# A planned FP32 kernel (attention with state, then two expert layers): the plan in eight passes by deadlines, turns of w3 in a stream of their own, rows of state row by row

## The chip, the cores and the metric

The kernel runs on one core of one Trainium2 chip. Five engines of that core matter here. PE is TensorE: it does the matrix products, and its weight loads are listed apart as PEld. DVE is VectorE. ACT is ScalarE. SP is SyncE, which here only issues DMAs. POOL does next to nothing. Each engine works off its own list of instructions strictly in order, and an instruction that waits holds up all that stand behind it on the same engine.

The metric is device time in microseconds (us) of one execution. Before the change three runs gave 1343.75, 1333.1 and 1341.79 us, so the median is 1341.79 us. The profile below is of one further execution, which took 1337.37 us.

## What is computed

```
# x 8x8x512x64, state 8x8x32x64, all FP32
scores  = x @ state^T / 8 ;  a  = softmax(scores)  (over the 32 rows of state)
xread   = a @ state                                # 512 rows of each batch
scores2 = state @ x^T / 8 ;  a2 = softmax(scores2) (over the 512 rows of x)
sread   = a2 @ x                                   # 32 rows of each batch
x = concat(xread, sread)  ->  4608 rows (8 batches of 544) x 512
x = ((x @ w1) * (x @ w2)) @ w3 @ w_out             # 512 -> 1024 -> 1024 -> 512
h = x @ w_in ;  g = h - tanh(h) ;  out = g @ w_out2   # 512 -> 2048 -> 512
```

FP32 accuracy is kept by splitting a number into a high and a low part and taking three products of parts (high-high, high-low, low-high). The weights of the layers come as 64-bit floats, so each slice of a weight has to be unpacked to FP32 by ACT and DVE before it is used.

## The kernel before

**Two parts.** The first part, to about 584 us of the span, does the attention, the first layer and all unpacking of weights. Its instructions are put in order by a planner (class `Plan`, L44 to L141). The second part, from there to the end, is the second layer; its order is written out by hand (`stage3`, `stage4`, `curve`, `finish`).

**What the first part does.** The words used below are these.

- *Products of w3.* `w3 @ w_out` is made first, in 16 steps t = 0 to 15 (8 for each half h of w3's rows). A step has a *turn* (`w3_turn`: four 128x128 transposes on PE into a PSUM bank), a *copy* of the bank to SBUF by ACT (the tile `w3t`), and a *product* (`w3_mul`: four matmuls, L735, which add into the banks acc0 to acc3). After steps 7 and 15 ACT and DVE take the four banks out as high and low part (`w3o`).
- *Unpacking.* A slice takes two ACTIVATEs (`unpack_abs` L261 and `unpack_tail` L267; the second is on DVE for every other slice of w3) and three DVE instructions (L278, L283, L289). The slices of w1 and w2, in four pairs kk = 0 to 3 (`raw12`, `dt12`), are then split into high and low part (`w12`). The memory of the pairs kk = 2 and 3 is that of the unpacked w_out, which the products of w3 read: pair 2 can be fetched only when product 11 is done, pair 3 only when product 15 is.
- *Folds.* Instead of x @ w1 with the x that attention reads, the rows of state are multiplied into w1 and w2 (`fold` r, kk, q: six matmuls on PE into two banks; r = 0 for batches 0 to 3, r = 1 for 4 to 7). ACT and DVE copy the banks out (`fe`), SP stores them in DRAM (`mdr`), and later loads them as `m` for each batch b and step k (`load_m`, a ring of three).
- *Attention of batch b.* `scores` on PE, then softmax steps on ACT and DVE, `et` (transposes) and `sr` (products) on PE. They give `at[b]`. The 32 rows of state of each batch go through `srb`, a transpose `st` on PE and a copy `keep_sr` (L535) into the tile `xsr`; after batch 7, `xsr` is split into `atsr`, the block b = 8.
- *Stage 1 and stage 2.* For b in 0 to 6, 8, 7 and k in 0 to 7, stage 1 multiplies `at[b]` by `m` (PSUM banks `ab`, two units a step), ACT and DVE make `ac` and `ph` of them, and stage 2 multiplies `ph` by `w3o` (banks acc0 to acc3, named y, two units of two banks a step). After k = 7 ACT copies the four banks to `y`, and SP stores them to DRAM (`ydr`), where the second part fetches them. The rings of `ac` and `ph` are two and three, that of `y` is two.

**What sets the order.** Each piece of work is a *part* with an engine, an assumed duration, what it needs, what buffers it takes and gives back. Parts stand in streams; in a stream the parts of one engine stay in order. `run` (L119) walks once through all streams: it works out when each engine's next part of every stream could start, takes the engine with the earliest start, and among that engine's parts that could start within 250 ns of it takes the one whose stream has the lowest rank for this engine. Turn, copy and product of w3 stand in one stream (`x_s`, rank 3 on PE and 2 on ACT), so on PE turn t + 1 follows product t. Buffers in four PSUM banks are picked by the same walk.

## Time and profile before

| | before |
|---|---|
| median of three runs | 1341.79 us (1333.1 to 1343.75) |
| the profiled execution | 1337.37 us, span 1335.5 us |
| PE busy | 1282.8 us (96% of the span) |
| DVE busy | 978.2 us (73%) |
| ACT busy | 723.9 us (54%) |
| mean granted TensorE clock | 0.993 |
| bytes moved | 150.58 MB, mean 113 GB/s |

The span is what the profiler recorded from the first to the last instruction; 1.9 us of the execution's time lie outside it. Busy time of an engine is the sum of its instructions. An engine's idle time ahead of an instruction is put down to what released that instruction ("releaser"). Where PE is busy nearly all the time, work on the other engines costs nothing as long as it is ready when PE comes to it.

### The profile page before, as it was taken

What the parts mean: (1) busy time and instruction counts of PE and PEld (TensorE: products, weight loads), DVE (VectorE), ACT (ScalarE), POOL (GpSimd) and SP (SyncE); (2) the same over time, 40 slices, a digit from 0 to 9 for tenths busy, and PEclk for the clock granted to TensorE, in tenths of its full rate; (3) what the DMA queues carried; (4) which work ended last, traced back from release to release, by engine and by line L of the source; (5) the groups of instructions that cost most, each with busy time, mean ns of one, the idle gap of its engine ahead of it and who ended that gap; (6) DMA issues with size and microseconds to landing.
All of it is one profiled execution on the core that took longest, in us unless ns stands there. A gap on an engine that the chain in (4) does not pass through costs nothing.

```text
span 1335.5 us, 17513 instructions
## 1 busy us (share of the span) xinstructions
PE 1282.8 (96%) x6416; PEld 1005.6 (75%) x6416; DVE 978.2 (73%) x1638; ACT 723.9 (54%) x1172; POOL 0.7 (0%) x6
## 2 busy tenths in 40 slices
PE   6798999999999999999999999999999999999996
PEld 3345676767777689788888888888888888888886
DVE  7898786775655842559977687787876877768775
ACT  7788575564646622446555455454544545545454
...
GB/s 326 270 226 212 255 256 214 246 200 280 250 250 284 189 91 95 220 69 90 1 64 1 9 56 0 64 0 1 64 0 54 10 1 64 1 0 48 1 32 16
DMA packets 98286, 150.58 MB, mean 113 GB/s; under 512 B 13976, under 2 KB 68248, under 8 KB 96152
## 3 DMA queue, kind: packets, MB, share of 16 engines
...
## 4 chain that ended last, share of the span: by engine, by line
PE 73%; DMA 12%; DVE 5%; ACT 4%; SPq 4%; issue 1%; DVEq 0%; ACTq 0%
PE h_ps L250 26%; PE o_ps L1286 26%; PE ab_ps L250 9%; PE y_ps L1027 7%; DMA raw_w<-in_moe_w_in_dram 3%; DMA m<-mdr 2%; DMA raw_p<-in_moe_w_dram 2%; PE w3o_ps L735 2%; DMA raw_w<-in_moe_w_out_dram 1%; DMA mdr<-fe 1%; SPq L396 1%; SPq L974 1%; PE m_ps L877 1%; DMA raw_p<-in_moe_w_out_dram 1%; ACT raw L267 1%
## 5 line engine op out<-in xcount | busy, mean ns | idle before, releaser
L250 PE MATMUL h_ps<-yt,w2in 128*128 128x512 f32 (+1 forms) x1728 | 394.0, 377 | 0.0
L250 PEld LDWEIGHTS h_ps<-yt,w2in 128*128 128x128 f32 x1728 | 313.4, 188 | 61.1
L250 PE MATMUL ab_ps<-at,m 128*128 128x512 f32 x768 | 196.2, 404 | 14.1 <-ACT ac L220 4.2
L1027 PE MATMUL y_ps<-ph,w3o 128*128 128x512 f32 (+1 forms) x864 | 201.4, 381 | 3.0 <-ACT y L220 3.0
L250 PEld LDWEIGHTS ab_ps<-at,m 128*128 128x128 f32 x768 | 141.6, 191 | 60.0 <-ACT ac L220 13.9
L1027 PEld LDWEIGHTS y_ps<-ph,w3o 128*128 128x128 f32 x864 | 153.7, 188 | 39.4 <-issue 6.1
L223 DVE TENSOR_TENSOR ph<-ac,ph 128x512 fp32r<-128x512 f32 (+1 forms) x72 | 47.5, 660 | 85.8 <-ACT ph L220 84.8
L220 ACT ACTIVATE ph<-ac 128x512 fp32r<-128x512 f32 (+1 forms) x72 | 43.9, 610 | 104.6 <-PE y_ps L1027 91.7
L735 PE MATMUL w3o_ps<-wo,w3t 128*128 128x512 f32 x128 | 64.0, 646 | 12.6 <-ACT w3t L220 12.6
L735 PEld LDWEIGHTS w3o_ps<-wo,w3t 128*128 128x128 f32 x128 | 24.7, 203 | 43.0 <-issue 26.5
L1010 DVE TENSOR_TENSOR ac<-ab_ps,ac 128x512 f32<-128x512 f32 (+1 forms) x72 | 47.2, 655 | 4.7 <-PE ab_ps L250 4.5
L267 ACT ACTIVATE raw_w<-raw_w 128x512 uint16<-128x512 uint32 x32 | 43.6, 1362 | 0.6
L220 ACT ACTIVATE ac<-ab_ps 128x512 f32<-128x512 f32 (+1 forms) x72 | 40.4, 561 | 2.0 <-PE ab_ps L250 1.9
L1296 DVE COPY ob<-o_ps 128x512 f32<-128x512 f32 x17 | 11.8, 692 | 39.1 <-PE o_ps L1286 39.1
L261 ACT ACTIVATE dt_w<-raw_w 128x512 f32<-128x512 f32 x32 | 21.4, 668 | 32.0 <-DMA raw_w<-in_moe_w_in_dram 16.6
L223 DVE TENSOR_TENSOR m<-m 128x512 fp32r<-128x512 f32 x32 | 22.0, 688 | 22.3 <-ACT m L220 22.0
L220 ACT ACTIVATE fe<-m_ps 128x512 fp32r<-128x512 f32 (+1 forms) x48 | 28.1, 601 | 16.8 <-PE m_ps L877 7.6
L220 ACT ACTIVATE m<-m 128x512 fp32r<-128x512 f32 x32 | 20.2, 631 | 30.2 <-DMA m<-mdr 30.0
L220 ACT ACTIVATE ob<-o_ps 128x512 f32<-128x512 f32 x17 | 10.2, 599 | 45.0 <-PE o_ps L1286 45.0
L877 PE MATMUL m_ps<-w,uu 64*128 64x512 f32 x192 | 32.3, 427 | 2.0 <-DVE fe L900 1.2
L278 DVE TENSOR_SCALAR dt_w<-dt_w 128x512 f32<-128x512 f32 x32 | 13.4, 420 | 23.4 <-ACT dt_w L261 23.2
L877 PEld LDWEIGHTS m_ps<-w,uu 64*128 64x128 f32 x192 | 16.8, 184 | 16.8 <-issue 6.2
...
## 6 DMA issues: line engine op xcount, KB each, us to landing
...
m<-mdr SPq DMA_DIRECT2D x128, 128.0 KB, 4.6
xb<-in_x_dram SPq DMA_DIRECT2D x64, 128.0 KB, 3.6
...
m<-mdr SPq DMA_DIRECT2D x128, 64.0 KB, 2.7
...
```

Source lines behind the costliest of these rows:

```text
L220: nc.scalar.activation(dst, src, AF.Copy)
L223: nc.vector.tensor_tensor(out=lo, in0=src, in1=hi.bitcast(F32), op=ALU.subtract)
L250: nc.tensor.matmul(out_ap, lhs(i), rhs(j), start=(n == 0), stop=(n == m - 1))
L261: nc.scalar.activation(t.bitcast(F32), w[:, :, 1].bitcast(F32), AF.Abs)
L267: nc.scalar.activation(tail, w[:, :, 0], AF.Copy, scale=TAIL)
L278: nc.vector.tensor_scalar(out=t, in0=t, scalar1=EXP_LO, scalar2=EXP_HI, op0=ALU.max, op1=ALU.min)
L396: nc.sync.dma_start(xb[b][band(q, j), j].rearrange("p g c d -> p g (c d)"), x[b, 2 * q + j].rearrange("(g p c) d -> p g (c d)", p=NS, c=NC),)
L735: nc.tensor.matmul(acc[a], v[:, a * P:(a + 1) * P], wo[j][:, 512:].bitcast(F32), start=(j == 0), stop=(j == nj - 1),)
L877: nc.tensor.matmul(ts[j].rearrange("p (k f) -> p k f", k=2), uu[r][1][d, i, q * P:(q + 1) * P], w[d, :, l, q, :], start=(n == 0), stop=(n ...
L1010: nc.vector.tensor_tensor(out=ab[b, k], in0=ab[b, k, 1], in1=ab[b, k], op=ALU.mult)
L1027: nc.tensor.matmul(acc[o][:, :n], w3o[k // 4][:, k // 2 % 2, i, c + o * P:c + (o + 1) * P], p[:, j], start=(k == 0 and e == 0), stop=(k == ...
L1286: nc.tensor.matmul(acc[t], g[:, i, t * P:(t + 1) * P], w[:, l, c], start=(f == 0 and e == 0), stop=(f == NF - 1 and e == 2),)
```

## The change

There are three edits.

1. **The plan is made eight times.** The old `emit` is split into `place`, which notes the times of a part and what it had to wait for, and the issue of the instructions, which now comes at the end. A pass (`order`) is the old walk, with one difference: among the parts that can start within 250 ns, the one with the earliest *deadline* (`late`) goes first. In the first pass the deadlines are the old ranks. After each pass `justify` goes through the parts from the last to the first and pushes each as late as the parts behind it and the free time of its engine allow; these times are the deadlines of the next pass. Of the eight passes the one in which PE ends first, by the planner's assumed durations, is issued.
2. **Turns and copies of w3 get a stream of their own** (`t3_s`), with ranks a little ahead of those of the products, so that a turn can be put ahead of the product of the step before.
3. **The rows of state lie row by row.** `keep_sr` writes the 128 x 128 numbers of a batch to every eighth place of `xsr` instead of to a block, and the last output DMA of each group of 128 rows names rows of state first and batches second. The number of instructions and of bytes stays the same.

The number of instructions on each engine is the same before and after, except that runs of equal rows join differently. The diff, cut to its core:

```
--- before.py
+++ after.py
@@ -46,32 +46,39 @@
 
 
 
+
+
     NEAR = 250.0
     REACH = {"PE": 200.0, "ACT": 130.0, "DVE": 130.0, "SP": 0.0}
+    ROUNDS = 8
 
     def __init__(self):
-        self.free = dict.fromkeys(self.REACH, 0.0)
-        self.moved = 0.0
-        self.made, self.slots, self.held, self.streams = {}, {}, {}, []
-
-        self.banks = [([0, 0.0], None) for _ in range(4)]
+        self.rings, self.streams = {}, []
+
         self.most = {"ab": 4, "w3x": 4, "fold": 2, "ps": 2}
         self.picked = []
 
     def ring(self, name, n):
-        self.slots[name] = (n, [])
+        self.rings[name] = n
 
     def stream(self, rank, ahead=16):
         s = {"rank": rank, "ahead": ahead, "parts": []}
         self.streams.append(s)
         return s["parts"]
+
+    def clear(self):
+        self.free = dict.fromkeys(self.REACH, 0.0)
+        self.moved = 0.0
+        self.made, self.held = {}, {}
+        self.slots = {name: (n, []) for name, n in self.rings.items()}
+        self.banks = [([0, 0.0, []], None) for _ in range(4)]
 
     def start(self, p):
         t = self.free[p["eng"]]
         for n in p["need"]:
             if n not in self.made:
                 return None
-            t = max(t, self.made[n])
+            t = max(t, self.made[n][0])
         for name, _, _ in p["take"]:
             if name in self.most:
                 continue
@@ -92,53 +99,109 @@
             t = max(t, free[want - 1])
         return t
 
-    def emit(self, p, t):
+    def place(self, p, t):
+
         end = t + p["dur"]
         self.free[p["eng"]] = end
         if p["bytes"]:
             self.moved = max(self.moved, t + 600) + p["bytes"] / 300.0
             end = self.moved + 1600
         reach = end + self.REACH[p["eng"]]
+        p["after"] = [q for n in p["need"] for q in self.made[n][1]]
+        p["span"], p["lag"], p["banks"] = (t, t + p["dur"]), reach - t - p["dur"], []
         for name, key, uses in p["take"]:
-            slot = [uses, 0.0]
+            slot = [uses, 0.0, []]
             if name in self.most:
                 k = min((b[0][1], i) for i, b in enumerate(self.banks) if not b[0][0])[1]
+                p["after"] += self.banks[k][0][2]
                 self.banks[k] = (slot, name)
-                self.picked.append(k)
+                p["banks"].append(k)
             else:
-                self.slots[name][1].append(slot)
+                n, given = self.slots[name]
+                if len(given) >= n:
+                    p["after"] += given[len(given) - n][2]
+                given.append(slot)
             self.held[key] = slot
         for key in p["give"]:
             slot = self.held[key]
             slot[0] -= 1
             slot[1] = max(slot[1], reach)
+            slot[2].append(p)
         for n in p["make"]:
-            self.made[n] = max(self.made.get(n, 0.0), reach)
-        p["fn"]()
-
-    def run(self):
-        while True:
+            at, by = self.made.get(n, (0.0, []))
+            self.made[n] = (max(at, reach), by + [p])
+
+    def order(self):
+        self.clear()
+        found, lists = [], [list(s["parts"]) for s in self.streams]
+        while any(lists):
             can = []
-            for s in self.streams:
+            for s, parts in zip(self.streams, lists):
                 seen = set()
-                for k, p in enumerate(s["parts"][:s["ahead"]]):
+                for k, p in enumerate(parts[:s["ahead"]]):
                     if p["eng"] not in seen:
                         seen.add(p["eng"])
                         t = self.start(p)
                         if t is not None:
-                            rank = s["rank"].get(p["eng"], 9) if p["rank"] is None else p["rank"]
-                            can.append((t, rank, s["parts"], k, p))
+                            can.append((t, p["late"], parts, k, p))
             if not can:
-                left = [s["parts"][0] for s in self.streams if s["parts"]]
+                left = [parts[0] for parts in lists if parts]
                 assert not left, [(p["eng"], p["need"], p["take"]) for p in left]
-                return
             t0, _, _, _, p0 = min(can, key=lambda c: c[0])
             t, _, parts, k, p = min(
                 (c for c in can if c[4]["eng"] == p0["eng"] and c[0] <= t0 + self.NEAR),
                 key=lambda c: (c[1], c[0]),
             )
             del parts[k]
-            self.emit(p, t)
+            self.place(p, t)
+            found.append(p)
+        return found
+
+    def justify(self, found):
+
+        end = max(p["span"][1] for p in found)
+        gaps = {e: [(0.0, end)] for e in self.REACH}
+        bound = {id(p): end for p in found}
+        for s in self.streams:
+            last = {}
+            for p in s["parts"]:
+                if p["eng"] in last:
+                    p["after"].append(last[p["eng"]])
+                last[p["eng"]] = p
+        late = {}
+        for p in sorted(found, key=lambda p: -p["span"][1]):
+            free = gaps[p["eng"]]
+            k = next(
+                (
+                    k for k in reversed(range(len(free)))
+                    if min(free[k][1], bound[id(p)]) - free[k][0] >= p["dur"]
+                ),
+                0,
+            )
+            a, b = free[k]
+            t = min(b, bound[id(p)]) - p["dur"]
+            free[k:k + 1] = [(a, t), (t + p["dur"], b)]
+            late[id(p)] = t
+            for q in p["after"]:
+                lag = q["lag"] if q["eng"] != p["eng"] or q["bytes"] else 0.0
+                bound[id(q)] = min(bound[id(q)], t - lag)
+        for p in found:
+            p["late"] = late[id(p)]
+
+    def run(self):
+        for s in self.streams:
+            for p in s["parts"]:
+                p["late"] = s["rank"].get(p["eng"], 9) if p["rank"] is None else p["rank"]
+        best = None
+        for _ in range(self.ROUNDS):
+            found = self.order()
+            end = max(p["span"][1] for p in found if p["eng"] == "PE")
+            if best is None or end < best[0]:
+                best = end, [(p, p["banks"]) for p in found]
+            self.justify(found)
+        for p, banks in best[1]:
+            self.picked += banks
+            p["fn"]()
 
 
 @with_exitstack
@@ -534,7 +597,7 @@
 
             def keep_sr():
                 copy(
-                    xsr[:, :, b * NS:(b + 1) * NS],
+                    xsr.rearrange("p q (n b) -> p q n b", b=B)[:, :, :, b],
                     s["st"].rearrange("p (q n) -> p q n", q=KT),
                 )
 
@@ -667,6 +730,7 @@
         w12, raws, f32s, acc_w = {}, {}, {}, {}
         w3o, w3v, w3x = {}, {}, {}
         w_s = plan.stream({"ACT": 3, "DVE": 3, "SP": 0}, 40)
+        t3_s = plan.stream({"PE": 2.8, "ACT": 1.5, "DVE": 1.5}, 40)
         x_s = plan.stream({"PE": 3, "ACT": 2, "DVE": 2, "SP": 0}, 40)
         d_s = plan.stream({"PE": 4, "ACT": 4, "DVE": 4, "SP": 1}, 24)
 
@@ -776,11 +840,11 @@
                 )
             whole = [("f32", i, n) for n in range(2 if i < 2 else 1)]
             part(
-                x_s, "PE", 4 * TURN, later(w3_turn, t), whole[:1], [("w3x", t)],
+                t3_s, "PE", 4 * TURN, later(w3_turn, t), whole[:1], [("w3x", t)],
                 [("w3x", ("w3x", t), 1), ("w3t", ("w3t", t))], [("pdt", i)] if h else (),
             )
             part(
-                x_s, "ACT", ("scalar", 512), lambda t=t: copy(w3v[t], w3x[t]),
+                t3_s, "ACT", ("scalar", 512), lambda t=t: copy(w3v[t], w3x[t]),
                 [("w3x", t)], [("w3t", t)], (), [("w3x", t)],
             )
             part(
@@ -1297,9 +1361,10 @@
             else:
                 copy(ob[:, t], acc[t])
             if j == B:
-                nb = P // NS
+
+                c = S + t * (P // B)
                 nc.sync.dma_start(
-                    out.rearrange("(b s) o -> b s o", b=B)[nb * t:nb * (t + 1), S:], ob[:, t]
+                    out.rearrange("(b s) o -> s b o", b=B)[c:c + P // B], ob[:, t]
                 )
         if j < B:
             nc.sync.dma_start(
```

What the change moves is shown at three places, in rows of the built programs: line, operation, what is written, what is read, size, and how many equal ones follow each other.

On PE at the start of the program: `w3_ps` t is the bank of turn t, `w3o_ps0` 0 to 3 are the four banks of the products, `w3t` t is the turned tile. Before:

```order
L242 MATMUL w3_ps1_201<-ident_74,wo0_125 128x128 x4
L735 MATMUL w3o_ps0_0_177<-wo0_125,w3t1_206 128x512
L735 MATMUL w3o_ps0_1_179<-wo0_125,w3t1_206 128x512
L735 MATMUL w3o_ps0_2_181<-wo0_125,w3t1_206 128x512
L735 MATMUL w3o_ps0_3_183<-wo0_125,w3t1_206 128x512
L242 MATMUL w3_ps2_234<-ident_74,wo0_125 128x128 x4
```

Of the changed kernel:

```order
L305 MATMUL w3_ps1_204<-ident_74,wo0_125 128x128 x4
L305 MATMUL w3_ps2_229<-ident_74,wo0_125 128x128 x4
L799 MATMUL w3o_ps0_0_181<-wo0_125,w3t1_209 128x512
L799 MATMUL w3o_ps0_1_183<-wo0_125,w3t1_209 128x512
L799 MATMUL w3o_ps0_2_185<-wo0_125,w3t1_209 128x512
L799 MATMUL w3o_ps0_3_187<-wo0_125,w3t1_209 128x512
L305 MATMUL w3_ps3_250<-ident_74,wo0_125 128x128 x4
```

Turn 2 stands ahead of product 1 now, and so it goes on: turn t + 1 is ahead of product t up to product 6, and turns 8 to 11 are ahead of product 8.

On ACT around the unpacking and splitting of pair 3 of w1 and w2 (`raw12_6`, `dt12_7` are its slices, `w12_3` its split form; `fe0_2` are copies of folds, `ac`, `ph`, `m`, `a`, `e2t` as in the words above). Before:

```order
L267 ACTIVATE raw12_6_944<-raw12_6_944 128x512
L474 ACTIVATE a1_1_893<-a1_1_893 128x512
L220 ACTIVATE ph0_2_1116<-ac0_2_1094 128x512
L220 ACTIVATE e2t1_1_1119<-et_ps1_1_996 128x512
L220 ACTIVATE fe0_2_301_1128<-m_ps0_2_3_0_1107 128x512
L220 ACTIVATE w12_3_1130<-dt12_6_1005 128x4x128 x2
L220 ACTIVATE w12_3_1130<-dt12_7_1053 128x4x128 x2
```

Of the changed kernel:

```order
L283 ACTIVATE fe0_2_001_954<-m_ps0_2_0_0_907 128x512
L330 ACTIVATE raw12_6_800<-raw12_6_800 128x512
L283 ACTIVATE fe0_2_101_976<-m_ps0_2_1_0_956 128x512
L283 ACTIVATE ph0_1_987<-ac0_1_941 128x512
L283 ACTIVATE w12_3_992<-dt12_6_898 128x4x128 x2
L283 ACTIVATE fe0_2_201_1003<-m_ps0_2_2_0_978 128x512
L283 ACTIVATE w12_3_992<-dt12_7_944 128x4x128 x2
```

Before, ACT has taken up step 2 of batch 0 (`ph0_2`) by then, and step 3 follows; now it is at step 1 (`ph0_1`). On PE the changed kernel has, between product 15 and the first fold of pair 3, only folds 0_1 and 0_2 (eight), scores of batch 1 and stage 1 of steps 0 and 1 of batch 0 (four units); before, stage 1 of steps 0 to 3 and five units of stage 2 stand ahead of that fold too.

On PE where the rows of state of batch 7 are turned (`st_ps7`) and the block b = 8 begins (`ab_ps8`). Before:

```order
L242 MATMUL st_ps7_4697<-ident_74,srb7_4693 128x128
L250 MATMUL ab_ps6_6_0_4699<-at6_4322,m6_6_4543 128x512 x6
L250 MATMUL ab_ps6_6_1_4714<-at6_4322,m6_6_4543 128x512 x6
L250 MATMUL ab_ps6_7_0_4726<-at6_4322,m6_7_4574 128x512 x6
L250 MATMUL ab_ps6_7_1_4739<-at6_4322,m6_7_4574 128x512 x6
L1027 MATMUL y_ps6_0_4590<-ph6_2_4514,w3o0_418 128x512 x3
```

Of the changed kernel:

```order
L579 MATMUL sr_ps7_1_4786<-xn7_4056,e2t7_1_4771 32x64 x16
L1091 MATMUL y_ps6_0_4517<-ph6_7_4711,w3o1_1078 128x512 x3
L1091 MATMUL y_ps6_1_4521<-ph6_7_4711,w3o1_1078 128x512 x3
L1091 MATMUL y_ps6_2_4550<-ph6_7_4711,w3o1_1078 128x512 x3
L1091 MATMUL y_ps6_3_4554<-ph6_7_4711,w3o1_1078 128x512 x3
L305 MATMUL st_ps7_4836<-ident_74,srb7_4833 128x128
L313 MATMUL ab_ps8_0_0_4849<-atsr_4839,w12_0_456 128x256 x12
L313 MATMUL ab_ps8_0_1_4863<-atsr_4839,w12_0_456 128x256 x12
```

Before, seven units of batch 6 stand between `st_ps7` and `ab_ps8`; now nothing does.

## Rows read from the trace of the kernel before

**Rows 1.** Windows: from:to, us, then busy us (instructions) of PE, PEld, DVE, ACT, POOL; PEclk, DMA share, GB/s

```profile
112.78:138.46 25.68, 24.28 (x166) 17.54 (x166) 24.00 (x47) 20.41 (x34) 0.00 (x0) 1.00 0.70 228
138.46:583.70 445.24, 426.47 (x2491) 328.50 (x2491) 273.98 (x512) 232.45 (x393) 0.00 (x0) 0.99 0.70 209
583.70:1335.50 751.80, 741.74 (x3361) 617.10 (x3359) 585.54 (x921) 386.75 (x634) 0.00 (x0) 1.00 0.08 28
```

**Rows 2.** Waits, whole span: who waited for whom, us in total, times, longest

```profile
PE w3o_ps L735 <- ACT w3t L220: 12.6, 13, 4.2
```

**Rows 3.** Waits of PE from 138.46 to 583.7 us, same columns

```profile
PE ab_ps L250 <- ACT ac L220: 4.2, 6, 1.8
PE y_ps L1027 <- ACT y L220: 3.0, 2, 1.7
PE ab_ps L250 <- ACT at L220: 1.7, 1, 1.7
```

**Rows 4.** Timeline of PE: start, us, line, operation, tiles, count (idle before, releaser)

```profile
15.28 3.70 PE L735 MATMUL w3o_ps<-wo,w3t 128*128 128x512 f32 x8 [0.69 <-ACT w3t L220]
18.91 0.66 PE L242 MATMUL w_ps<-ident,wo 128*128 128x128 f32 x4
...
48.39 5.40 PE L735 MATMUL w3o_ps<-wo,w3t 128*128 128x512 f32 x8 [4.22 <-ACT w3t L220]
...
96.44 0.97 PE L877 MATMUL m_ps<-w,uu 64*128 64x512 f32 x6
97.34 1.95 PE L421 MATMUL sc_ps<-xt,ut 32*32 32x512 f32 x32
...
108.75 0.96 PE L877 MATMUL m_ps<-w,uu 64*128 64x512 f32 x6
...
131.08 0.65 PE L516 MATMUL sr_ps<-xn,e2t 128*32 128x64 f32 x32
...
138.46 0.96 PE L877 MATMUL m_ps<-w,uu 64*128 64x512 f32 x6
```

**Rows 5.** Timeline of PE, later: two units of stage 1; turn of batch 7's rows

```profile
384.26 3.06 PE L250 MATMUL ab_ps<-at,m 128*128 128x512 f32 x12
...
480.52 0.27 PE L242 MATMUL st_ps<-ident,srb 128*128 128x128 f32 x1
```

**Rows 6.** Timeline of ACT: unpacking of the first slices of w1, w2; two copies

```profile
44.06 0.68 ACT L261 ACTIVATE dt<-raw 128x512 f32<-128x512 f32 x1 [4.08 <-DMA raw<-in_moe_w_dram]
44.77 1.34 ACT L267 ACTIVATE raw<-raw 128x512 uint16<-128x512 uint32 x1
45.85 0.69 ACT L261 ACTIVATE dt<-raw 128x512 f32<-128x512 f32 x1
...
56.29 0.60 ACT L220 ACTIVATE w3t<-w_ps 128x512 f32<-128x512 f32 x1
56.78 0.59 ACT L220 ACTIVATE sc<-sc_ps 128x512 f32<-128x512 f32 x1
```

**Rows 7.** Timeline of DVE: end of w3's third slice; low parts of pair 3

```profile
17.62 1.23 DVE L289 SCALAR_TENSOR_TENSOR wo<-raw_p,wo 128x1024 uint32<-128x1024 uint32 x1 [2.47 <-ACT raw_p L267]
...
130.83 2.49 DVE L223 TENSOR_TENSOR w<-dt,w 128x512 fp32r<-128x512 f32 x4
```

**Rows 8.** Windows of product 7 and of four units after 451.9 us, columns as in Rows 1

```profile
48.39:53.72 5.33, 5.33 (x8) 2.03 (x9) 4.62 (x10) 5.07 (x7) 0.00 (x0) 0.68 1.09 348
...
451.90:456.42 4.52, 4.52 (x15) 3.28 (x13) 3.87 (x8) 1.87 (x4) 0.00 (x0) 0.62 1.03 376
```

**Rows 9.** The tile xsr: what writes and reads it; ns min/median/max, first and last start us

```profile
L220 ACT ACTIVATE xsr<-st_ps x8: 266/278/283, 78.5 to 481.7; 128x128 f32<-128x128 f32 x8
...
L223 DVE TENSOR_TENSOR atsr<-xsr,atsr x2: 686/690/694, 482.7 to 483.3; 128x512 fp32r<-128x512 f32 x2
```

**Rows 10.** DMA issues of the page: count, KB each, us to landing

```profile
m<-mdr SPq DMA_DIRECT2D x128, 128.0 KB, 4.6
```

**Rows 11.** The chain that ended last, in order of time: start, us, what

```profile
372.24 9.41 DMA m<-mdr
```

## The prediction

> **What bounds the kernel now.** I first cut the span into windows by what PE does [rows 1]. From 583.70 us to the end PE is busy 741.74 of 751.80 us. This is the second layer; its order is written by hand and the diff leaves it alone. So nothing is won there, and the 751.8 us stay. What the change can move lies before 583.7 us. From 138.46 to 583.70 PE is busy 426.47 of 445.24 us, so 18.8 us are idle while DVE (274) and ACT (232) have room: PE bounds that stretch, and its idle time is many small waits. From 112.78 to 138.46 DVE is busy 24.00 of 25.68 us and PE 24.28: there PE and DVE are both near full.
>
> Next I read who PE waits for. The largest sum is the products of w3 waiting for the copy of their own turn: 13 waits, 12.6 us [rows 2]. The timeline shows the pattern: a product of 3.63 us (15.28 to 18.91), a turn of 0.66, a wait of 0.69 for ACT; the longest such wait is the 4.22 us before the product at 48.39 [rows 4]. That product also ran slowly, 5.33 us at a mean granted clock of 0.68 [rows 8], so for most of it at 1.2 instead of 2.4 GHz: 1.7 us more than the one at 15.28. The four units of 451.90 (4.52 us at 0.62) did the same after a wait, against 3.06 us for as many matmuls at 384.26 [rows 5, 8]. In the later stretch the waits of stage 1 for `ac`, of stage 2 for `y` and for `at` are the largest [rows 3].
>
> **The sum, step 1: products 0 to 7.** Turn t + 1 now stands ahead of product t, so the copy has a whole product's time, and the 0.69 us go. At the start this costs something: product 1 waits behind turn 2, which needs w3's third slice. That slice's last DVE instruction began at 17.62 after waiting 2.47 us for ACT, which stood behind a copy [rows 7]; without the copy it can begin near 15.2, but the data of the next slices come in order, and I take turn 2 at 17.0. Then product 1 is at 17.7, product 2 at 17.7 + 3.63 + 0.66 = 22.0, and products 2 to 7 with a turn each take 6 x 4.29 = 25.7: product 7 ends at 47.7. Before it ended at 48.39 + 5.33 = 53.7. Gain here 6.0 us, 1.7 of them the clock.
>
> **Step 2: products 8 to 15.** PE's list up to product 15 is eight products (29.0), seven turns (4.6), scores of batch 0 (1.95), four folds (3.9), two et as long as a turn (1.3), two sr (1.3) and st (0.3): 42.3 us [rows 4, 5]. Waits: the fourth matmul of product 8 needs acc3 taken out, which on ACT stands behind four unpacked slices (44.06 + 4 x (0.71 + 1.08) + 5 copies x 0.49 + a low part of 0.7 = 54.4 [rows 6, 9]), when PE is there at 47.7 + 3 turns + 1.95 + 2.7 = 54.3; and turn 12 comes about 1.8 us before its slice is through. I take 2 us. Product 15 ends at 47.7 + 42.3 + 2 = 92.0; before at 108.75.
>
> **Step 3: the folds, where most of this is given back.** Pair 3 of w1 and w2 can be fetched only after product 15. Before, it was split 130.83 + 2.49 - 108.75 = 24.6 us later [rows 4, 7]. The same path (fetch, eight ACT instructions, three times four on DVE, the split) now starts at 92.0 and ends at 116.6. The order puts the first fold of pair 3 on PE behind only eight folds (7.8), scores (1.95) and four units of stage 1 (6.1), 15.9 us, so PE stands about 9 us. By 119.5 it has done that fold, an et and one more fold (0.97 + 0.66 + 0.97, 0.3 of waiting). Before, PE at 138.46 had done four units of stage 1 and five of stage 2 more (9 x 1.53 = 13.8), an et and two sr more (2.0), and two folds less (1.9): the same state as now at 138.46 - 13.9 = 124.6. **Gain up to here 5.1 us**, out of 16.7 at product 15. Bounds: 14 if the pair is ready as PE comes; 0 if ACT and DVE need 5 us more.
>
> The Trainium skill says in "Perfetto Trace Analysis", Optimization Strategy, that where the most-contended engine changes over time, interleaving the regimes may help. The new order does the opposite here: it packs the folds together, ahead of most of stages 1 and 2, and the trace has ACT and DVE full in that stretch [rows 1]. What this would do in full is rival B.
>
> **Step 4: 138.46 to 583.70.** The same instructions run for the same times; only waits can go, 18.8 us in all. Two I can follow. Stage 2 of batch 4 began on banks that `y` copies had not left (1.7 us); four units of stage 1 now stand between. Batch 6's stage 1 followed its last sr directly and waited for `at` (1.7) [rows 3], and then ran 4.52 - 3.06 = 1.5 us longer at the low clock; `at` has far more time now. That is 4.9 us. Of the other 15.4 us I cannot say which the new order removes. None is the one bound, all the other; I take a third, 5.1, since of what I could follow nearly all goes, but stage 1's waits for `ac` come from ACT's long unpacking in between, which stays. Against it stands a new wait: after `st` of batch 7 PE goes straight to block 8. Before, from `st` at 480.52 to the end of the last low part at 483.3 + 0.69 it took 3.5 us, hidden behind seven units [rows 5, 9]; now PE stands for it. **Gain 4.9 + 5.1 - 3.5 = 6.5 us**; bounds 1.4 and 16.8.
>
> **What costs nothing.** `keep_sr` writes strided: 8 x 0.28 us on ACT [rows 9]. Were each twice as long, 2.2 us on an engine with 213 us free would be covered, but the last lies in the 3.5 us above (0.3). The output DMA of the rows of state moves the same rows of 2 KB. SP issues as many DMAs as before, with unpacked slices of the second layer's weights fetched somewhat earlier and `m` between them (rival C).
>
> **Sum.** 1337.4 - 5.1 - 6.5 = 1325.8, rounded to **1325 us**. It is made against the profiled execution (span 1335.5 and 1.9 outside it), which is 4.4 us below the median of the three runs; 1% is about 13.4 us, about what a measurement of this kernel can tell from no change.
>
> **The rivals.** *B: the front's gain is given back and the rest only changes place.* If pair 3 comes 5 us later, step 3's gain is 0; if new waits replace the old ones in step 4, as the one at `st` does, step 4 gives 0 too: 1331 to 1341, about 1336. For it: PE is 95.8% busy in that stretch already, DVE is full in the folds. Against it: 4.9 us of named waits go.
>
> *C: the loads of `m` come too late, and the kernel is slower.* A load takes 4.6 us [rows 10], the longest piece on the chain 9.41 [rows 11]. Its slot comes free when stage 1 of three steps before ends; two steps of stages 1 and 2 (8 units x 1.53 = 12.2 us) cover load, copy and low part (1.3). So it decides from 10.9 us on: if the fetches that are now earlier hold every load at 11.4, each of 64 steps costs 0.5, 32 us less the gains: about 1355. Against it: the median is half that.
>
> *D: nearly all waits go.* Step 3 gives 10, step 4 its 16.8: about 1311. For it: eight passes look for just these waits. Against it: the planner's durations are fixed, the chip's ACT and DMA are not.
>
> **How the numbers follow.** Forecast (A, 1316 to 1333) 0.50, B 0.28, C 0.08, D 0.14. The range from 1309 to 1342 holds A, B and most of D; C and the edge of D, about 0.13, lie outside. Faster by over 1% begins near 1326 (between 1% under the profiled execution, 1324, and under the median, 1328): D and six tenths of A lie below, 0.14 + 0.30 = 0.44. Slower by over 1% is C, 0.08. The rest, 0.48, is within 1%.
>
> **What would show it.** Step 1: product 7 ends near 48 at full clock, and `w3t` is gone from PE's waits. Step 2: product 15 ends near 92. Step 3: a wait of about 9 us, in pieces, before the first fold of pair 3 near 117. Step 4: PE idle for some 3 us ahead of `ab_ps8`, and the first part's idle time after pair 3 near 12 us; the second layer begins near 572. If it begins at 583, B held, and the waits will stand in other lines; if `m` loads show 10.9 us or more, C.

## The result and the profile after

The changed kernel takes 1324.05 us (median, 1321.34 to 1325.83); the kernel before takes 1338.35 us beside it. The ratio is 0.9895 with a 95% interval from 0.9874 to 0.9917: 14 us, about 1.05%. The profiled execution is 1323.79 us long with a span of 1322.0, against 1337.4 and 1335.5 before.

The total is what was forecast, the parts are not. The span is 13.5 us shorter. 5.1 us of that lie behind PE's last product, and 8.4 us ahead of the second layer, which begins at 575.17 instead of 583.55. The prediction cuts the stretch ahead of it once more, at a point of equal work that it puts at 124.6 in the kernel before; the changed kernel is there at 124.15. By that point 0.4 us are won in front of it and 8.0 us behind it. The point itself is put right below, with the steps of the prediction.

The products' wait for their own turn is gone, as two rows of the page show (busy us and mean ns of one, then the idle time ahead of it and its releaser; before, the copy of the turn ended 12.6 us of waits [rows 2]):

```profile
L799 PE MATMUL w3o_ps<-wo,w3t 128*128 128x512 f32 x128 | 60.0, 614 | 1.2 <-ACT w3t L283 1.1
L941 PE MATMUL m_ps<-w,uu 64*128 64x512 f32 x192 | 35.0, 446 | 9.4 <-DVE fe L964 4.4
```

The second row is where much of that time went: the folds now wait 9.4 us; in the kernel before it was 2.0. PE's timeline of the front shows it in order (start, duration, operation, in brackets the wait and who ended it), to be read against [rows 4]:

```profile
41.16 3.60 PE L799 MATMUL w3o_ps<-wo,w3t 128*128 128x512 f32 x8
...
49.31 2.43 PE L484 MATMUL sc_ps<-xt,ut 32*32 32x512 f32 x32 [3.25 <-DVE ut L441]
51.67 7.52 PE L799 MATMUL w3o_ps<-wo,w3t 128*128 128x512 f32 x16
...
83.11 7.13 PE L799 MATMUL w3o_ps<-wo,w3t 128*128 128x512 f32 x16 [0.25 <-ACT w3t L283]
...
95.32 2.06 PE L941 MATMUL m_ps<-w,uu 64*128 64x512 f32 x12 [1.41 <-ACT fe L283]
...
98.49 2.57 PE L313 MATMUL ab_ps<-at,m 128*128 128x512 f32 x10 [0.45 <-DVE m L286]
...
104.38 0.96 PE L941 MATMUL m_ps<-w,uu 64*128 64x512 f32 x5 [2.90 <-DVE fe L964]
...
110.73 0.96 PE L941 MATMUL m_ps<-w,uu 64*128 64x512 f32 x5 [0.43 <-DVE ac L1074]
112.24 1.50 PE L941 MATMUL m_ps<-w,uu 64*128 64x512 f32 x6 [0.54 <-DVE fe L964]
114.75 0.97 PE L941 MATMUL m_ps<-w,uu 64*128 64x512 f32 x6 [1.01 <-DVE fe L964]
118.05 0.80 PE L941 MATMUL m_ps<-w,uu 64*128 64x512 f32 x2 [2.33 <-ACT w L283]
119.14 1.22 PE L941 MATMUL m_ps<-w,uu 64*128 64x512 f32 x4 [0.29 <-DVE w L286]
120.29 1.11 PE L305 MATMUL et_ps<-ident,sc 128*128 128x128 f32 x4
121.33 0.79 PE L941 MATMUL m_ps<-w,uu 64*128 64x512 f32 x1
122.58 1.64 PE L941 MATMUL m_ps<-w,uu 64*128 64x512 f32 x5 [0.45 <-ACT fe L283]
```

Product 7 ends at 41.16 + 3.43 = 44.6, product 15 at 90.2; before at 53.7 and 108.75. Then PE waits seven times before the first fold of pair 3, which begins at 118.05, and the folds behind that run slowly: six matmuls of a fold take 0.97 us at 114.75, and 0.80 + 1.22 from 118.05. DVE's last part of the split of pair 3 ends at 117.20 + 1.88 = 119.08; its timeline:

```profile
117.20 1.88 DVE L286 TENSOR_TENSOR w<-dt,w 128x512 fp32r<-128x512 f32 x3
```

By stretches (length, then busy us of PE, PEld, DVE, ACT and POOL, the granted clock, the DMA share):

```profile
90.17:124.15 33.98, 24.11 (x121) 13.19 (x121) 27.79 (x51) 27.62 (x44) 0.00 (x0) 0.83 0.83 238
124.15:490.30 366.15, 356.71 (x2131) 269.87 (x2130) 256.89 (x490) 207.79 (x349) 0.00 (x0) 1.00 0.77 231
490.30:497.13 6.83, 5.53 (x23) 5.05 (x24) 1.29 (x2) 2.90 (x6) 0.00 (x0) 0.58 0.52 146
497.13:575.17 78.04, 76.64 (x461) 68.05 (x459) 28.76 (x44) 27.45 (x50) 0.00 (x0) 0.99 0.39 118
```

After 124.15 PE is idle for 9.4 + 1.3 + 1.4 = 12.1 us, where the kernel before had 18.8 us in the corresponding stretch [rows 1]. The largest wait left there is at `st` of batch 7 and block 8 behind it. PE's timeline:

```profile
485.65 3.06 PE L1091 MATMUL y_ps<-ph,w3o 128*128 128x512 f32 x12
490.30 0.33 PE L305 MATMUL st_ps<-ident,srb 128*128 128x128 f32 x1 [1.60 <-DVE srb L589]
491.78 8.39 PE L313 MATMUL ab_ps<-atsr,w 128*128 128x256 f32 x42 [1.15 <-ACT atsr L283]
```

DVE's timeline ahead of it:

```profile
487.76 0.71 DVE L554 STREAM_TRANSPOSE at<-a 128x512 f32<-128x512 f32 x1
...
489.17 0.69 DVE L286 TENSOR_TENSOR at<-at,at 128x512 fp32r<-128x512 f32 x1 [0.46 <-ACT at L283]
489.78 0.47 DVE L589 TENSOR_SCALAR srb<-sr_ps,r 128x64 f32<-128x64 f32 x2
```

`sr` left PE at 485.7, but `srb` stands on DVE behind the second softmax's `at`, which nobody needs yet. PE waits 2.75 us, and the next 6.8 us run at a mean clock of 0.58.

### The profile page after: what moved, and what is told of

Its sections match the earlier page's. It is cut to its first block, busy times and chain, and to the rows that moved or that the text cites. A ratio compares the mean times of both kernels' runs of the same rounds, so it can differ in the third digit from the quotient of the medians.

```text
span 1322.0 us, 17523 instructions
## 1 busy us (share of the span) xinstructions
PE 1280.2 (97%) x6416; PEld 1010.0 (76%) x6416; DVE 978.6 (74%) x1638; ACT 723.4 (55%) x1172; POOL 0.7 (0%) x6
## 4 chain that ended last, share of the span: by engine, by line
PE 73%; DMA 6%; DVE 6%; ACT 2%; SPq 2%; issue 1%; DVEq 0%; ACTq 0%
PE h_ps L313 27%; PE o_ps L1350 26%; PE ab_ps L313 10%; PE y_ps L1091 8%; DMA w2dr_out<-dt_w 2%; DMA m<-mdr 2%; SPq L1038 1%; DMA w2dr_in<-dt_w 1%; PE m_ps L941 1%; DMA mdr<-fe 1%; DMA raw_w<-in_moe_w_in_dram 1%; PE sc_ps L484 1%; SPq L971 0%; DMA w2lin<-w2dr_in 0%; ACT raw_w L330 0%
## 5 line engine op out<-in xcount | busy, mean ns | idle before, releaser
L799 PE MATMUL w3o_ps<-wo,w3t 128*128 128x512 f32 x128 | 60.0, 614 | 1.2 <-ACT w3t L283 1.1
L941 PE MATMUL m_ps<-w,uu 64*128 64x512 f32 x192 | 35.0, 446 | 9.4 <-DVE fe L964 4.4
L283 ACT ACTIVATE fe<-m_ps 128x512 fp32r<-128x512 f32 (+1 forms) x48 | 28.5, 607 | 13.5 <-DMA mdr<-fe 7.3
L341 DVE TENSOR_SCALAR dt_w<-dt_w 128x512 f32<-128x512 f32 x32 | 13.5, 421 | 29.4 <-ACT dt_w L324 29.4
```

The costliest lines, as they stand in the source:

```text
L283: nc.scalar.activation(dst, src, AF.Copy)
L341: nc.vector.tensor_scalar(out=t, in0=t, scalar1=EXP_LO, scalar2=EXP_HI, op0=ALU.max, op1=ALU.min)
L799: nc.tensor.matmul(acc[a], v[:, a * P:(a + 1) * P], wo[j][:, 512:].bitcast(F32), start=(j == 0), stop=(j == nj - 1),)
L941: nc.tensor.matmul(ts[j].rearrange("p (k f) -> p k f", k=2), uu[r][1][d, i, q * P:(q + 1) * P], w[d, :, l, q, :], start=(n == 0), stop=(n ...
```

## The experiments

**Edit 3 alone (the rows of state).** The kernel before, with the two hunks on `xsr` and on the output DMA:

```diff
-                    xsr[:, :, b * NS:(b + 1) * NS],
+                    xsr.rearrange("p q (n b) -> p q n b", b=B)[:, :, :, b],
...
-                    out.rearrange("(b s) o -> b s o", b=B)[nb * t:nb * (t + 1), S:], ob[:, t]
+                    out.rearrange("(b s) o -> s b o", b=B)[c:c + P // B], ob[:, t]
```

> The kernel before with the third edit alone (rows of state row by row: keep_sr strided, the last output DMAs by rows first). Theory L (the end): after the last product the changed kernel's span ended 4.8 us after PE instead of 9.9, so the edit shortens the last two output DMAs; expected here: the stretch from PE's last product to the span's end falls from 9.9 to about 4.9 us, the time by about 5 us (1338.4 to 1333.4, ratio 0.996), nothing else moves except that each of the eight keep_sr copies takes 0.42 us instead of 0.28. Theory P (the prediction's): the edit costs nothing and gives nothing; expected: 1338 us, ratio 1.000, and the end stays at 9.9 us.

Measured: 1332.58 us, ratio 0.9969 (0.9952 to 0.9985). PE's last product ends at 1326.5 (before at 1325.6), the span 4.8 us later instead of 9.9. Theory L holds: about a third of the whole gain comes from this edit, and all of it from the end.

**Why the end is shorter.** The kernel before, with the pattern of the last output DMA cut by hand into one DMA per batch:

```diff
-                nc.sync.dma_start(
-                    out.rearrange("(b s) o -> b s o", b=B)[nb * t:nb * (t + 1), S:], ob[:, t]
-                )
+                for i in range(nb):
+                    nc.sync.dma_start(
+                        out.rearrange("(b s) o -> b s o", b=B)[nb * t + i, S:], ob[i * NS:(i + 1) * NS, t]
+                    )
```

> The kernel before, with one edit: each of the last two output DMAs (128 rows of 2 KB, destination in 4 batches of 32 rows each) is issued as four DMAs of 32 rows, one batch each; the same rows go to the same places. Edit 3 alone shortened the end (the span behind PE's last product) from 9.9 to 4.8 us. Theory P (the pattern: a destination whose outermost count is 4 keeps only a few of the 16 DMA engines busy, as the 2 to 3 tenths of the last 10 us of the kernel before suggest): each of the four DMAs has 32 rows as its outermost count, so the end is again near 4.8 plus the three more issues of about 0.5 us, 5 to 6.5 us, the DMA engines 6 to 9 tenths busy, and the whole about 4 us shorter, 1332 beside 1336, ratio 0.997. Theory A (the addresses: 32 rows lying side by side in memory land slowly): the end stays at 9.9 us or becomes longer, ratio 1.000.

Measured: 1334.27 beside 1338.07 us, ratio 0.997 (0.9948 to 0.9993); the span ends 5.9 us after the last product. The rows of the DMA engines' mean busy share over the last 23 to 26 us show it, each digit the tenths in one fortieth. Of the kernel before:

```profile
DMA  0000000000000000000000000032122222221000
```

Of the changed kernel:

```profile
DMA  0000000000000000000010000000000078940000
```

Of the kernel with four DMAs:

```profile
DMA  0000000010000000003557553000000000000000
```

Before, 2 to 3 tenths of 16 engines are busy for 7 us, which is what 3 to 5 engines working alone would give; after, 7 to 9 tenths for 2 us; with four DMAs, which SP issues one after the other, 3 to 7 tenths for 4 us. The same views count the packets. Beside the 256 rows of 2 KB there are small ones (under 512 B). The three rows are of the kernel before (two DMAs), of the changed kernel (two) and of the kernel with four DMAs for each of the two (eight):

```profile
DMA packets 266, 0.55 MB, mean 21 GB/s; under 512 B 8, under 2 KB 8, under 8 KB 264
DMA packets 289, 0.54 MB, mean 24 GB/s; under 512 B 32, under 2 KB 32, under 8 KB 288
DMA packets 385, 0.54 MB, mean 22 GB/s; under 512 B 128, under 2 KB 128, under 8 KB 384
```

That is 4, 16 and 16 small packets per DMA. By the packets' own times in the traces, 4 rows are under way at once for 5.3 of the 7.2 us before and mostly 15 to 17 in the changed kernel, and one takes 84 ns (median) in both. The bytes and the addresses are the same, and in this experiment the 32 rows of a batch still lie side by side, so it is the pattern, as theory P has it: a destination of 4 x 32 rows occupies few engines, by these counts 4, one of 16 x 8 or of 32 rows many, by these counts 16. The Trainium skill has the rule, in "DMA: Bandwidth & Descriptors", section "Why a DMA increments its semaphore by 16 and not by 1": a DMA uses the largest number of engines up to 16 that divides the slowest dimension of both sides. By that rule 4 engines before and 16 after; the counts of 4 and 16 agree.

**Edit 2 alone (turns in a stream of their own, one pass).**

```diff
+        t3_s = plan.stream({"PE": 2.8, "ACT": 1.5, "DVE": 1.5}, 40)
...
-                x_s, "PE", 4 * TURN, later(w3_turn, t), whole[:1], [("w3x", t)],
+                t3_s, "PE", 4 * TURN, later(w3_turn, t), whole[:1], [("w3x", t)],
...
-                x_s, "ACT", ("scalar", 512), lambda t=t: copy(w3v[t], w3x[t]),
+                t3_s, "ACT", ("scalar", 512), lambda t=t: copy(w3v[t], w3x[t]),
```

> The kernel before with the second edit alone (turns and copies of w3 in a stream of their own; one pass by ranks). Theory F (the front's gain is lost at the folds whatever the plan): product 15 ends some 10 to 16 us earlier than 108.75, the w3t waits (12.6 us) fall under 3 us, but the second layer begins at most 3 us earlier than 583.6, so 1335 to 1339 us. Theory P (the prediction's step 3): about 5 us of the front's gain stay, 1333 us; the second layer begins near 578.

Measured: 1342.24 us, ratio 1.0042 (1.0027 to 1.0058): slower than before, although product 15 ends at 89.9. PE's rows right behind:

```profile
100.97 1.65 PE L878 MATMUL m_ps<-w,uu 64*128 64x512 f32 x6 [3.33 <-DVE fe L901]
106.45 1.64 PE L878 MATMUL m_ps<-w,uu 64*128 64x512 f32 x5 [3.83 <-ACT fe L220]
```

The folds wait for the copies that empty their banks, and from 95 to 110 us the mean clock is 0.56. Theory F has the mechanism, but not that more is lost than was won: the second layer begins at 588.75, 5 us later than before. And PE waits at `st` of batch 7 and ahead of block 8, which it does not in the kernel before:

```profile
505.40 0.33 PE L242 MATMUL st_ps<-ident,srb 128*128 128x128 f32 x1 [1.60 <-DVE srb L526]
507.10 13.18 PE L250 MATMUL ab_ps<-atsr,w 128*128 128x256 f32 x83 [1.37 <-ACT atsr L220]
```

**Edit 1 alone (eight passes).** The changed `Plan` with the turns back in `x_s` and the old rows of state:

```diff
-        t3_s = plan.stream({"PE": 2.8, "ACT": 1.5, "DVE": 1.5}, 40)
...
-                t3_s, "PE", 4 * TURN, later(w3_turn, t), whole[:1], [("w3x", t)],
+                x_s, "PE", 4 * TURN, later(w3_turn, t), whole[:1], [("w3x", t)],
...
```

> The kernel before with the first edit alone (eight passes by deadlines; turns stay in the stream of the products, rows of state as before). Theory F: the gain of the plan lies behind the folds, so this alone takes the second layer's begin from 583.6 to about 576 (1331 us), with the w3t waits still near 12 us. Theory P: without the turn stream the passes lack the front's 5 us, and the begin is near 579 (1334 us).

Measured: 1335.98 us, ratio 0.9998 (0.9978 to 1.0018). Neither theory has it: the second layer begins at 582.4, where 576 and 579 were expected. Product 15 ends at 111.6 and the products still wait 13.7 us for their turns: within `x_s` the order on PE is fixed, and passes can't move a turn past a product.

**Edits 1 and 2 without 3.** The changed kernel with the two lines of edit 3 put back:

```diff
-                    xsr.rearrange("p q (n b) -> p q n b", b=B)[:, :, :, b],
+                    xsr[:, :, b * NS:(b + 1) * NS],
...
```

> The changed kernel without its third edit (both edits of the plan, rows of state as before). Theory L: the second layer begins at 575.2 as in the changed kernel, the end after PE's last product is 9.9 us again, and the time is 5 us above the changed kernel's: 1329 us, ratio to before 0.993. Theory P: same as the changed kernel, 1324 us, ratio 0.989.

Measured: 1327.15 us, ratio 0.9939 (0.992 to 0.9959), and the end is 9.9 us again: theory L. Alone, the passes bring nothing and the turns cost 0.4%; together they bring 0.6%. Where that arises is seen by cutting at 125 us (PE busy is the first number after the length). The kernel before:

```profile
90.00:125.00 35.00, 30.57 (x179) 17.13 (x178) 31.11 (x59) 28.80 (x47) 0.00 (x0) 0.95 0.75 233
125.00:583.55 458.55, 439.78 (x2580) 337.96 (x2579) 286.23 (x534) 241.33 (x409) 0.00 (x0) 0.99 0.70 208
```

The turns alone:

```profile
90.00:125.00 35.00, 25.49 (x138) 15.23 (x138) 30.94 (x57) 29.91 (x48) 0.00 (x0) 0.80 0.79 240
125.00:588.75 463.75, 440.90 (x2608) 340.40 (x2607) 287.74 (x538) 242.69 (x411) 0.00 (x0) 0.99 0.68 207
```

Both:

```profile
90.00:125.00 35.00, 25.95 (x124) 14.98 (x124) 29.30 (x55) 28.31 (x46) 0.00 (x0) 0.79 0.85 246
125.00:572.11 447.11, 438.77 (x2610) 342.36 (x2610) 285.31 (x534) 237.20 (x403) 0.00 (x0) 0.99 0.70 211
```

| kernel | product 15 ends | PE busy 0 to 125 | PE idle from 125 to the second layer | second layer begins |
|---|---|---|---|---|
| before | 108.75 | 101.1 | 18.8 | 583.55 |
| turns alone | 89.9 | 100.3 | 22.9 | 588.75 |
| passes alone | 111.6 | 100.6 | 18.6 | 582.4 |
| both | 90.4 | 102.6 | 8.3 | 572.1 |
| all three | 90.2 | 100.2 | 12.1 | 575.2 |

Wherever product 15 ends, PE has been busy about 101 us at 125: whatever the products win, the folds lose. (Slow matmuls count in full as busy, and the mean clock from 0 to 125 is 0.97, 0.95, 0.97, 0.93 and 0.95 in the order of the table, so with the turns in a stream of their own a little less work is done by then.) The kernels differ in the idle time behind that. The last two rows have the same order on every engine and are 3 us apart at the second layer, so much a single profiled execution scatters here.

**The wait at `st` of batch 7.** The changed kernel, with the parts of the last batch listed in another order (`by_rows` is the loop of `sum1` to `lo`, without `whole2` for that batch):

```diff
+            if b < B - 1:
+                by_rows()
+            else:
+                for j in range(G):
+                    p("DVE", 330, whole2, (j,), [("e", j)], [("r2", j)])
...
                     p("DVE", full, sr_lo, (q,), [("srh", q)], [("atsr", q)])
+                by_rows()
```

> The changed kernel, with one edit in batch 7's attention alone: its DVE parts for the rows of state (whole2, srtake, then turn, keep_sr and the split) are listed ahead of the sums, products and splits of its second softmax (sum1 to lo), which block 7 needs only after block 8. In the changed kernel PE waits 1.60 us for srb and 1.15 for atsr at 490.3 us, and the 8 us from 490 run at a granted clock of 0.59, 3.4 us of them lost to it. Theory S (the queue: srb stands behind at on DVE, and the clock fell because PE stood): both waits and the slow 6.8 us go, block 8 begins near 488.8, the second layer near 569 instead of 575.2, and the whole is about 6 us shorter, 1318, ratio to the kernel before 0.985. Theory M (the wait only moves: to the copies of y, to atsr or to at of batch 7): the second layer begins at 573 to 576, 1322 to 1325, ratio 0.989. If the clock falls there anyway: about 3 us, 1321.

Measured: 1318.88 us, ratio 0.9858 (0.9834 to 0.9882). PE's timeline at that place:

```profile
488.19 0.27 PE L305 MATMUL st_ps<-ident,srb 128*128 128x128 f32 x1
488.21 1.65 PE L1100 MATMUL y_ps<-ph,w3o 128*128 128x512 f32 x6
489.69 0.33 PE L313 MATMUL ab_ps<-atsr,w 128*128 128x256 f32 x1
490.37 9.88 PE L313 MATMUL ab_ps<-atsr,w 128*128 128x256 f32 x81 [0.34 <-DVE atsr L286]
```

Of 2.75 us of waits 0.34 are left, the clock stays up, and the second layer begins at 569.7. Theory S holds: the wait was worth 5 us, and it comes from the order of DVE's list, which no pass can change since the order within a stream is fixed. It came in with the turns and not with the passes: the turns alone have it (1.60 and 1.37 us, above), the passes alone do not, since there seven units stand between `st` at 479.49 and block 8 at 489.19. A pass can hide such a wait; the plan that was issued did not.

**The stores of the folds on a queue of their own.** One word of the changed kernel:

```diff
-            nc.sync.dma_start(
+            nc.gpsimd.dma_start(
                 mdr[r, kk][q, :, :, l, j * 256:(j + 1) * 256], fes[r, kk, q, j, l].bitcast(F32)
```

> The changed kernel, with one edit: the stores of the folds (fe to mdr) are issued from POOL's queue instead of SP's; every other instruction stands where it stood on every engine. In the changed kernel ACT and DVE wait for a free fe buffer, that is for a store, before they can empty a fold's bank (2.17 us before the copy at 103.64), and PE waits 2.90 us for that at 104.38, with a slow clock from 104.8 on; six stores are issued at 107.8 to 113.9 behind eight loads of xb, which take SP 7.33 us. Theory Q (the queue: stores stand behind loads in SP's order): the waits of ACT and DVE for stores mostly go, PE's waits for fe between 95 and 118 fall from 8 to about 4 us, the slow 3.41 us at 104.8 go, and the point that the changed kernel reaches at 124.15 comes 4 to 6 us earlier: about 1319, ratio to the kernel before 0.985. Theory B (the DMA engines, 82% busy from 88 to 126, are what is short): the stores land as late, the same waits stay, 1323 to 1325, ratio 0.989. If a store issued by POOL lands later than one issued by SP (3.7 us), the folds get slower: 1327 or more.

Measured: 1316.51 us, ratio 0.9844 (0.9821 to 0.9868). The time is that of theory Q, the place is not. In the front PE's timeline still shows waits for `fe`:

```profile
104.66 0.96 PE L941 MATMUL m_ps<-w,uu 64*128 64x512 f32 x5 [1.76 <-DVE fe L964]
...
114.59 0.97 PE L941 MATMUL m_ps<-w,uu 64*128 64x512 f32 x6 [1.69 <-DVE fe L964]
```

The point that the changed kernel reaches at 124.15 comes at 124.23, so there theory B was right. Since PE's order is the same in both, the starts of `st` of each batch tell where the gain lies: 147.50 and 147.87 for batch 1, 199.35 and 197.88, 265.65 and 263.32, 309.37 and 305.83, 351.00 and 345.85, 401.35 and 396.01, 490.30 and 484.11. 5.5 of the 6.2 us are won between 148 and 351 us; the second group of states is folded there, from 153 to 315. A store itself does not land sooner (median 4.8 us instead of 3.5). PE is idle for 3.1 of the 203 us from 148 to 351, instead of 6.5: a wait of 1.7 us of stage 1 on a copy of a fold and one of 1.0 for `ac` are gone. How the queue does that is not shown.

**The same with the turns alone.** The kernel of edit 2 alone, with the same word changed:

```diff
-            nc.sync.dma_start(
+            nc.gpsimd.dma_start(
                 mdr[r, kk][q, :, :, l, j * 256:(j + 1) * 256], fes[r, kk, q, j, l].bitcast(F32)
```

> The kernel before with edit 2 (turns of w3 in a stream of their own, one pass of the planner), and the stores of the folds issued from POOL's queue. With edit 2 alone it was slower than before (1.0042), with 3.8 and 3.3 us of waits of the folds for fe and 13.65 us of slow clock at 96. Theory Q (stores stand behind loads in SP's queue, and that is what takes the gain of products 8 to 15 back): those waits shrink below 3 us in all, and the time falls to the time before or under it, ratio 0.995 to 1.000. Theory B (DMA engines): ratio stays 1.003 to 1.005.

Measured: 1353.29 us, ratio 1.0109 (1.0078 to 1.0141), slower still, and by neither theory. PE's two waits are a little shorter and still there (1.91 and 3.37 us at 99.89 and 106.35, instead of 3.33 and 3.83). What is new is on SP's queue, here the sum, number and longest of its waits for stores from 76 to 156 us ahead of the loads of `m`, with the stores on SP (edit 2 alone):

```profile
SPq L975 <- DMA mdr<-fe: 3.4, 6, 0.8
```

With the stores on POOL:

```profile
SPq L975 <- DMA mdr<-fe: 28.0, 11, 6.6
```

With the stores off its queue SP runs ahead to loads of `m` that need them, and stands there with everything behind it. Whether that is the whole of the 9 us is not shown; the pair shows that the queue of the stores is worth 7 us for one order and costs 9 us with the other.

**Less of pair 3 on ACT.** Tails of two of its four parts (and of pair 2) on DVE, at the same place in the order:

```diff
-                lambda: unpack_tail(raw(), tail),
+                lambda: unpack_tail(raw(), on or tail),
...
+                    on="DVE" if kk > 1 and u % 2 else None,
```

> The changed kernel with one edit: of the four parts of pairs 2 and 3 of w1 and w2 that are unpacked, the second and the fourth have their tail (the 128x512 uint16) written by DVE instead of ACT, at the same place of the order. One takes ACT 1.35 us and DVE 0.73. In the changed kernel ACT is busy 27.6 of the 34 us from 90.17 to 124.15 and DVE 27.8, and PE waits 2.33 us for ACT's copy of pair 3 at 118.05. Theory A (ACT's list is the chain to pair 3): 2.7 us less on ACT for the pair, so its first fold begins near 115.5, the wait goes, and the whole is 2 to 4 us shorter, 1320 to 1322, ratio to the kernel before 0.987. Theory V (DVE is as full, and the fetch sets the pace): DVE gets 1.5 us more per pair and empties the folds' banks later, pair 3 comes no earlier than 117.5, 1324 or a little more, ratio 0.989 to 0.991.

Measured: 1324.17 us, ratio 0.9906 (0.9877 to 0.9934): no gain, theory V. The first fold of pair 3 begins at 118.52:

PE's timeline:

```profile
115.16 1.65 PE L942 MATMUL m_ps<-w,uu 64*128 64x512 f32 x6 [1.10 <-DVE fe L965]
118.52 0.80 PE L942 MATMUL m_ps<-w,uu 64*128 64x512 f32 x2 [1.71 <-ACT w L283]
```

PE's wait for ACT is shorter (1.71 instead of 2.33 us) and its waits for `fe` on DVE are longer (5.1 instead of 4.5 us from 90 to 118): from 90 to 124 us DVE is now busy for 30.5 of 34 us and ACT for 23.9, where it was 27.8 and 27.6 from 90.17 to 124.15, and work moved from one to the other wins nothing there. The execution that was profiled is the fastest of the six, 1317.37 us; the others took 1321.83 to 1329.66.

**Both gains together.** The two edits of the changed kernel that had helped, in one:

```diff
-            nc.sync.dma_start(
+            nc.gpsimd.dma_start(
                 mdr[r, kk][q, :, :, l, j * 256:(j + 1) * 256], fes[r, kk, q, j, l].bitcast(F32)
...
                     p("DVE", full, sr_lo, (q,), [("srh", q)], [("atsr", q)])
+                by_rows()
```

> The changed kernel with both edits that were tried alone: batch 7's rows of state ahead of its second softmax on DVE (alone 0.9858 of the time before, beside 0.9895 for the changed kernel), and the stores of the folds issued from POOL's queue (alone 0.9844). Theory S (two separate places: the stores' gain lies between 150 and 350 us, the other at 490, and with the stores alone the 2.7 us of waits at st of batch 7 and 6.8 us of slow clock behind them were still there): the gains add, 0.9895 - 0.0037 - 0.0051 = 0.981, 1312 to 1313. Theory O (one gain: both are mostly a new order or a shift of the same waits): 0.984 to 0.985, 1317. A ratio under 0.983 is for S.

Measured: 1311.15 us, ratio 0.982 (0.9792 to 0.9848): they add, as theory S has it, though the interval reaches into that of theory O. This is the fastest kernel here, 25 us under the one before beside it. PE is idle for 5.5 us from 125 to the second layer, which begins at 559.4; with one of the edits alone it was 9.2 and 8.9 us.

**The planner's costs.** This kernel with costs closer to the trace, and with larger ones:

```diff
-    "scalar": (180, 0.85), "tail": (206, 2.28), "vector": (150, 1.04), "twice": (150, 0.53),
+    "scalar": (70, 0.82), "tail": (0, 2.15), "vector": (60, 1.06), "twice": (180, 0.53),
```

> The kernel with both edits (rows of state of batch 7 first, stores on POOL's queue), and the planner's costs of ACT and DVE set to the spacing that the trace shows: scalar 70 + 0.82 ns per element instead of 180 + 0.85, tail 2.15 per element instead of 206 + 2.28, vector 60 + 1.06 instead of 150 + 1.04, twice 180 + 0.53 instead of 150 + 0.53; so the order alone changes. Theory T (the waits that are left come from durations that the planner has wrong): 3 to 6 us shorter than without, 1307 to 1310, ratio to the kernel before near 0.978. Theory E (the planner's order is one of many of equal worth, and what is left are loads, stores and the clock, which it does not know): within 3 us of the kernel without it, either way, ratio 0.979 to 0.984. The slower tails and copies that it now takes as shorter could also bring PE to waits it had hidden: over 1316.

```diff
+    "scalar": (240, 0.85), "tail": (260, 2.28), "vector": (210, 1.04), "twice": (210, 0.53),
```

> The kernel with both edits (ratio 0.982 to the kernel before), and 60 ns more in the planner's cost of every ACT and DVE instruction (scalar 240, tail 260, vector 210, twice 210 ns beside the part per element), where the costs set to the trace's spacing had brought 0.982 up to 1.0075. Theory R (what the planner's costs hold beyond the instructions is a reserve for loads, stores and queues that it does not know, and the more of it, the more work lies between a result and its use): 0.978 to 0.982. Theory E (any other order is a draw, and the eight passes had a good one): 0.982 to 0.992, with waits of other names in the same sum. Theory L (with longer costs ACT and DVE look full to the planner, which then starts folds and stages late): over 0.992.

Measured: 1347.13 us, 1.0075 (1.0047 to 1.0103), with the costs of the trace; 1317.82 us, 0.9872 (0.9845 to 0.9899), with the larger ones; 0.982 with those of the kernel. With the costs of the trace it is 2.6% slower than without them, so theories T and E are both out, and the third case that the expectation names has come. Its largest waits from 125 us to its second layer at 597.1:

```profile
PE ab_ps L313 <- ACT ac L283: 9.7, 6, 4.7
PE m_ps L950 <- DVE fe L286: 7.3, 5, 2.8
```

These are copies out of PE's banks by ACT and DVE. It fits that the planner now thinks them done sooner and sets their readers too close, so that part of the costs would be a reserve, but no run shows this by itself. More reserve doesn't help, and theory R is out: 0.9872 lies with that run's theory E. Between the three sets of costs the same passes scatter over 2.6%, which is more than the whole change gains (1.05%). So how much of the gain of edits 1 and 2 is the method of the passes, and how much one good order among many, stays open.

## Why the prediction was right in its sum and wrong in its terms

**Step 1** held: product 7 ends at 44.6 at full clock (47.7 was forecast), and of the 12.6 us that the products waited for `w3t` 1.1 are left. The start was taken too slow by 3 us.

**Step 2** held: 90.2 against 92.0. The 3 us of step 1 are in it; from product 7 to product 15 it took 45.6 us, where 44.3 were forecast. Two waits replace the 2 us, 3.25 for `ut` at 49.31 and 1.62 for a slice near 66.6.

**Step 3** had the right mechanism and a wrong size: by its own point of equal work 0.4 us instead of 5.1. The 9 us of waiting in pieces are there (1.41 + 0.45 + 2.90 + 0.43 + 0.54 + 1.01 + 2.33 = 9.07). But the path from product 15 to the end of the split of pair 3, taken over from the kernel before as 24.6 us, took 28.9 (90.17 to 119.08). So the first fold of pair 3 begins at 118.05, not 116.6, 1.45 us late, and even then it has only the high part; and from there to the next stage 1 it takes 6.1 us, not 2.9. At full clock the two folds and the et would have run 2.9 us less (folds of 2.02 and 2.43 instead of 0.97 us, an et of 1.11 instead of 0.66); the rest are waits of 0.29 and 0.45, where 0.3 was forecast. The clock from 90.17 to 124.15 is 0.83 on the mean; the kernel before has 0.95 from 90 to 125. So the step left out two things: that the path need not keep its length in the new order, and the slow clock that can follow waits, although the prediction had read just that in [rows 8]. Rival B's first half, the front given back, is what happened: the path is 4.3 us longer, where B had put 5. The Trainium skill's advice of "Perfetto Trace Analysis", Optimization Strategy, to interleave stages with different limits, fits that the folds packed together ran into ACT and DVE, but no run here interleaves them.

**The point of equal work** was misread as well. PE's timeline of the kernel before, ahead of 138.46:

```profile
135.97 0.97 PE L877 MATMUL m_ps<-w,uu 64*128 64x512 f32 x6
136.86 1.66 PE L1027 MATMUL y_ps<-ph,w3o 128*128 128x512 f32 x6
```

The first is its first fold of pair 3, the second a sixth unit of stage 2; the prediction counts five units and two folds less, which is the state at 135.97 and not at 138.46. With six units and one fold, at its own prices, the equal point is 138.46 - (10 x 1.53 + 2.0 - 0.97) = 122.1 instead of 124.6. With 1.41 us for a unit, as four of them follow each other from 384.26 to 389.88 in the kernel before, it is 123.3. So the front did not win 0.4 us but lost 0.8 to 2.0. Either is less than the 3 us that a single profile scatters, so nothing can be said to be won there; and the stretch behind won 9.2 to 10.4 us.

**Step 4** was right on the idle time: 12.1 us where near 12 was forecast, the waits for `y` and for `at` of batch 6 gone. That is 6.7 us less than before, against a forecast gain of 6.5. The rest of the 9.2 to 10.4 us was not foreseen. The step took PE's busy time as fixed, but up to the second layer it is 538.3 us instead of 540.9 (100.24 + 438.04 against 101.13 + 439.78), at a mean clock that is no higher; why stays open. The new wait at `st` is there with 2.75 us (3.5 was forecast). That its slow clock would follow was not foreseen; without the wait the kernel is 5 us faster. The second layer begins at 575.2 where 572 was forecast; the same order begins it at 572.1 in the kernel without edit 3, so this difference is no more than scatter.

**What was to cost nothing** is the step that failed outright, and with it the sentence that the 751.8 us behind the first part stay: they are 746.8. The strided copy of `keep_sr` costs 0.42 us instead of 0.28 [rows 9], off the path but for the last. But the output DMA, put at nothing since "the same rows of 2 KB" move, gave 5.1 us, and edit 3 alone shows it (0.9969). Nothing ran behind it: it is the last work of the kernel, so that its landing counted in full, and the prediction looked at its bytes and not at its pattern.

**The sum** is right by luck. Step 3 was taken 5.9 to 7.1 us too high, step 4 2.7 to 3.9 too low, and the end's 5.1 were left out: 1325.8 + 5.9 - 2.7 - 5.1 = 1323.9, the time of the profiled execution. The errors cancel, and the forecast of 1325 is 1 us off for that reason.

**The rivals.** C did not come: loads of `m` land in 4.6 us as before [rows 10], and none of PE's waits in the changed kernel ends with one (0.45 us at 98.49 ends with DVE's work on `m`). D, nearly all waits gone, is where one gets with two edits more: 5.5 us of idle time and 1311.15 us, its forecast time.
